# Gated linear attention and a multiplicative FFN on one core: q and k of chunks 2 to 8 issued by GpSimd, the decays' rows stored from ScalarE's queue

## The chip, the cores and the metric

The kernel runs on one core of a Trainium2 chip, as one launch. The metric is the device time of the launch in microseconds (us). A profile is one execution of its own. It names the engines PE (TensorE matmuls), PEld (TensorE weight loads), DVE (VectorE), ACT (ScalarE), POOL (GpSimd) and SP (SyncE, which here only issues DMAs). A "q" behind a name (SPq, POOLq) is that engine's instruction queue.

## The reference

The inputs are q, k, v and alpha of shape (batch 4, heads 8, 768 positions, 48 values), and four float64 weight matrices. The first half is a recurrence over the positions of each head, the second half a gated feed-forward layer with two further products:

```python
for t in range(S):
    state = alpha[:, :, t, :, None] * state + np.einsum('bhd,bhe->bhde', k[:, :, t], v[:, :, t])
    y[:, :, t] = np.einsum('bhd,bhde->bhe', q[:, :, t], state)
x = y.transpose(0, 2, 1, 3).reshape(B * S, H * D)      # (3072, 384)
out = ((x @ w1) * (x @ w2) @ w3) @ w_out               # (3072, 384)
```

## The kernel before

**Chunks.** The 768 positions of a batch are cut into 6 chunks of 128, so there are 24 chunks `n` = 0 to 23. A chunk's tile has the 128 positions on the partitions and 8 heads by 48 values along each partition. In memory, 48 values of one head at one position lie together (192 bytes), so each load of alpha, k, q or v of a chunk (192 KB) consists of 1,024 pieces of 192 bytes.

**What is done for a chunk.** `logs(n)` takes the logarithm of alpha on ScalarE (L272). `decays(n)` sums the logarithms over the positions with one matmul (L287) and makes two tiles `e` with Exp (L293, L294). `decayed(n)` multiplies k and q with them on VectorE (L303, tile `qk`). `transposed(n)` turns `qk` over on TensorE (L325), and ScalarE copies it out (L327, tile `qkT`). `scores(n)` multiplies keys and queries (L365), VectorE masks the product (L368, tile `ms`), `outer(n)` makes the chunk's contribution to the state (L337, added at L345 or L347), and `attend` and `attend_state` give y (L391, L385), which ScalarE copies out (L395, tile `x`) and SP stores to a scratch tensor `xd`.

**Rows for the state.** Between two pairs of chunks the state has to be decayed. For this, three rows of 384 values are stored to a small tensor `ends` in memory: a row of alpha (L279, in `logs`) and two rows of `e` (L296 and L298, in `decays`). `load_ends` reads them back as single values on partitions (L311, two DMAs, tile `dec`), and `advance` multiplies them together and onto the state on GpSimd (L354 to L356, tile `T`). This is done for chunks 2, 4, 8, 10, 14, 16, 20 and 22. All these DMAs are issued by GpSimd.

**Weights.** w1 and w2 come as float64 in tiles of 128 by 512 (`raw`, 512 KB, L192). `to_fp32` and `load_gates` convert a tile in several steps on ScalarE (L200, L205, L217) and VectorE (L201, L204, L207, L208, L210, L219). The first six tiles are needed before the first gate can start.

**Order of the work.** The loop over `n` (L600) writes one step per chunk. Step `n` holds the scores of chunk `n`, the transposes of `n + 1`, `decayed(n + 2)`, `decays(n + 3)` and `logs(n + 4)`; in the first six steps (`n < FIRST`) it also holds about one weight tile's conversion. Each engine works through its own instructions in order. A tile scheduler sets that order; `after_marks(...)` keeps an instruction behind a named one. `mark["pool"]` names an instruction of GpSimd behind which the loads of v are put. From step 5 on, the matmuls of the gates (L421, 18 or 9 at a time) are mixed in. A gate of the first group needs the first three chunks' `xd`, loaded as `xT` (L407) and split by `split_x` (L413 on ScalarE, L414 and L415 on VectorE), and the first six weight tiles. After the attention come the remaining gates, the product of w3 and w_out (the "fold") and the last product.

**Loads and their queues.** SP issues, in program order, alpha (L132), k and q (L138, L139), v of chunks 0 to 2 and from 8 on (L144), `raw` (L192), the stores of `xd` (L262) and more. GpSimd issues v of chunks 3 to 7. alpha and kq have three buffers each, so kq of chunk `n + 3` can start only when `decayed(n)` has read chunk `n`, and alpha of chunk `n + 3` only when `logs(n)`, and the store of alpha's row where there is one, have read chunk `n`. `raw` has four buffers. Each DMA signals its end on one of eight semaphores for the DMAs of SP and ScalarE, or of eight for those of GpSimd, taken in turn; so an issue waits until the DMA that had the same semaphore eight issues earlier has landed.

Of the kernel before, what the change touches and what calls it, by code (L numbers as in the profile page):

```python
# [48 lines left out]
def kernel(  # L49
# [12 lines left out]
    nc = tc.nc  # L62
    B, H, S, D = q.shape
    C = 128
# [5 lines left out]
    DP = 64  # L70
# [32 lines left out]
    def bank():  # L103
        return ps.tile([C, 512], FP32, tag="bank", name="bank")

    st, mark = {}, {}

    def after_marks(*names):
        stack = ExitStack()
        for x in names:  # L110
            stack.enter_context(tc.issue_after(mark[x]))
        return stack
# [4 lines left out]
    ends = {n: dram.tile([3, DM], FP32, name=f"ends{n}") for n in range(2, N, 2) if n % NCH}  # L117
# [7 lines left out]
    def rows(src, n):  # L125
        b, c = divmod(n, NCH)
        return src[b, :, ds(c * C, C), :].rearrange("h p d -> p h d")

    def load_a(n):
        if n < N:  # L130
            st["a", n] = inp.tile([C, H, D], FP32, tag="ac", name="ac")
            nc.sync.dma_start(out=st["a", n], in_=rows(alpha, n))  # L132

    def load_kq(n):
        if n >= N:
            return
        st["kq", n] = inp.tile([C, 2, H, D], FP32, tag="kq", name="kq")
        nc.sync.dma_start(out=st["kq", n][:, 0], in_=rows(k, n))  # L138
        nc.sync.dma_start(out=st["kq", n][:, 1], in_=rows(q, n))  # L139

    def load_v(n):
        if n < N:
            st["v", n] = vs[n % len(vs)]
            (nc.gpsimd if 2 < n < 8 else nc.sync).dma_start(out=st["v", n][:, :, 0:D], in_=rows(v, n))  # L144

    nc.scalar.preload_act_table_set(LN_EXP_SET)
    load_a(0)
# [20 lines left out]
    decs = [p1.tile([C, 3, NP], FP32, name=f"dec{i}") for i in range(2)]  # L168
# [68 lines left out]
    def fetch(ahead=3):  # L237
        while weights and len(begun) < ahead:
            begun.append(weights.popleft())
            next(begun[-1])  # L240
# [17 lines left out]
    def store():  # L258

        while later:  # L260
            dst, src = later.popleft()
            nc.sync.dma_start(out=dst, in_=src)  # L262
# [4 lines left out]
    def logs(n):  # L267
        if n >= N:
            return
        a = st.pop(("a", n)).rearrange("p h d -> p (h d)")  # L270
        la = st["la", n] = work.tile([C, DM], FP32, tag="la", name="la")
        nc.scalar.activation(la, a, AF.Ln)  # L272
        if n >= LATE:

            t = st["la", n] = work.tile([C, 2, DM], FP32R, tag="la2", name="la2", bufs=1)
            nc.scalar.copy(t[:, 0], la)
            nc.vector.tensor_sub(t[:, 1], la, t[:, 0].bitcast(FP32))
        if n in ends:
            nc.gpsimd.dma_start(out=ends[n][2:3], in_=a[0:1])  # L279

    def decays(n):
        if n >= N:
            return
        lc = bank()[:, 0:DM]
        la = st.pop(("la", n))
        if n < LATE:
            nc.tensor.matmul(lc, sums[:, n % 2].bitcast(FP32), la, start=True, stop=True)  # L287
        else:
            for i in range(2):
                nc.tensor.matmul(lc, sums[:, n % 2], la[:, i], start=(i == 0), stop=(i == 1))  # L290

        e = st["e", n] = work.tile([C, 2, DM], FP32, tag="e", name="e", bufs=3)
        nc.scalar.activation(e[:, 0], lc, AF.Exp, scale=-1.0)  # L293
        mark["e", n] = nc.scalar.activation(e[:, 1], lc, AF.Exp).ins  # L294
        if n in ends:
            mark["pool"] = nc.gpsimd.dma_start(out=ends[n][0:1], in_=e[0:1, 0]).ins  # L296
        if n + 1 in ends:
            mark["pool"] = nc.gpsimd.dma_start(out=ends[n + 1][1:2], in_=e[C - 1:C, 1]).ins  # L298
        load_ends(n)

    def decayed(n):
        if n < N:
# [3 lines left out]
    def load_ends(n):  # L306
        if n not in ends:
            return
        with nc.allow_non_contiguous_dma(reason="single values to partitions"):
            for i in range(2):  # L310
                nc.gpsimd.dma_start(out=decs[n // 2 % 2][ds(DP * i, D)].rearrange("d m j -> d (m j)"),  # L311
                                    in_=ends[n].rearrange("m (j i d) -> i d (m j)", i=2, d=D)[i])

    def transposed(n):
        if n >= N:
# [58 lines left out]
    def attend_state(n):  # L374
        qkT = st.pop(("qkT", n))

        y = [bank()[:, 0:HP * C].rearrange("p (j c) -> p j c", c=C) for _ in range(2)]
        st["y", n] = y, [(half * HP + j, i, y[i][ds(DP * half, DP), j, :])  # L380
                         for j in range(HP) for i in range(2) for half in range(2)]
        if n % NCH:
            for j, i, to in st["y", n][1]:
                r = ds(DP * i, D)
                nc.tensor.matmul(to, Ts[n % 2][r, j, :], qkT[r, 1, j, :],  # L385
                                 start=(j % HP == 0), stop=False, skip_group_check=True)
# [18 lines left out]
    def load_x(g, queue=nc.sync):  # L405
        st["xT", g] = xp.tile([C, KM, TG], FP32, tag="xT", name="xT")
        queue.dma_start(out=st["xT", g], in_=xd[g].rearrange("(k p) t -> p k t", p=C))  # L407

    def split_x(g, i):
        x = st.pop(("xT", g))  # L410
        t = tr[i].tile([C, 3, KM, TG], FP32R, tag="x3", name="x3")
        st["x3", g] = t
        nc.scalar.activation(t[:, 0], x, AF.Copy, scale=1.0 - 2.0 ** -13)  # L413
        nc.vector.tensor_sub(t[:, 1], x, t[:, 0].bitcast(FP32))  # L414
        mark["x3"] = nc.vector.scalar_tensor_tensor(t[:, 2], t[:, 0].bitcast(FP32), -1.0 - 1.0 / P, x,  # L415
                                                    op0=ALU.mult, op1=ALU.add).ins
# [73 lines left out]
    def gate(g, f):  # L490
        yield from (late_gate if late else early_gate)(g, f)
# [104 lines left out]
    FIRST = 6  # L596
# [3 lines left out]
    for n in range(N + 1):  # L600
        store()
        if n in loads:
            load_x(loads[n])
        load_a(n + 5)
        raws = (3, 3, 3, 3, 2, 2, 3, 3)[n] if n < 8 else 4
        for m in (n + 3,) * (n <= FIRST) + (n + 4,) * (n >= FIRST):
            load_kq(m)
            if n < FIRST - 2:
                fetch(raws)
            if n >= FIRST:  # L610
                load_v(m - 1)
        if n:
            attend_state(n - 1)
        if n < N:
            scores(n)
        transposed(n + 1)
        if n < FIRST:
            with after_marks("pool"):
                load_v(n + 2)
        if n - 2 in begin and n > FIRST:  # L620
            g, tiles = begin[n - 2]
            with after_marks(("ms", n), ("qkT", n + 1)):
                split_x(g, 0)
            fill.extend(gate(g, f) for f in tiles)
        pieces = (3, 3, 2, 0)[(n - FIRST) % 4] if n >= FIRST else 0
        if n == 0:
            with after_marks(("qkT", 0)):
                logs(2)
            decays(2)
            with after_marks(("e", 2)):  # L630
                logs(3)
        early, ready = n < FIRST, len(thirds) if n > 2 else n // 2
        marks = (*[("qkT", n + 1)] * (n < N - 1), *[("qk", n + 1), ("ms", n)] * early, *["x3"] * (n - 2 in begin and n > FIRST))
        if n < N - 2:
            with after_marks(*marks):
                convert(2 if n == 0 else 1, raws)
        advance(n)
        if n:
            attend(n - 1)
        outer(n)  # L640
        third(ready)
        run(pieces > 0)
        if early:
            with after_marks(*marks):
                convert(1, raws)
        with after_marks(*[("ms", n)] * (n < 3)):
            decayed(n + 2)
        if not early:
            with after_marks(*[("qkT", n + 1)] * (n < N - 4)):
                logs(n + 4)  # L650
        if n == 4:
            load_x(0)
        convert(early and n > 0, raws)
        run(pieces > 1)
        decays(n + 3)
        if early:
            with after_marks(("e", n + 3)):
                logs(n + 4)
        if n < N - 2:
            convert(early or n % 3 == 0, raws)  # L660
        if n == FIRST - 1:
            assert len(done) == 2 * KM
            g, tiles = begin[n - 2]
            with after_marks("l"):
                split_x(g, 0)
            fill.extend(gate(g, f) for f in tiles)
        run(pieces > 2)
        if n == N - 3:
            while begun:
                convert(1)  # L670
            weights.extend(load_out(j) for j in range(KF))
            fetch(4)
# [91 lines left out]
```

## Time and profile before

| what | value |
|---|---|
| median of 3 runs | 476.67 us (474.95 to 478.01) |
| the profiled execution: its own time | 476.57 us |
| its span, first to last instruction | 474.8 us |
| PE busy | 456.5 us, 96% of the span |
| DVE, ACT, POOL busy | 359.1, 279.6, 76.6 us |
| DMA packets under 512 bytes | 99,360 of 148,783 |
| load of k or q of a chunk, 192 KB: issue to landing | 5.7 us in the median |
| load of `raw`, 512 KB: issue to landing | 5.2 us in the median |

The times of a profile count from the span's start. A "busy" engine is one with an instruction running; PE's busy time is modelled, since matmuls overlap. In the timeline view a row holds the start, the busy time, engine, line, operation, the tiles (written <- read), the count, and in brackets how long the engine had been idle before and what ended that. In the view of stages, a row gives each engine's busy time within a window, then the clock that TensorE was granted (1.00 is full), the share of time in which the 16 DMA engines had packets (packets overlap, so it can be over 1), and the rate in GB/s.

### The profile page before, as it was taken

Reading aid. Unit: us, or ns where it says so; the run is one execution under the profiler, and the core shown is the slowest. Engines: PE = TensorE matmul, PEld = TensorE weight load, DVE = VectorE, ACT = ScalarE, POOL = GpSimd, SP = SyncE. Lnnn points to the kernel's source line nnn. Section 1 sums busy time; section 2 is a strip of 40 time slices with the busy share of each in tenths; the row PEclk is TensorE's granted clock in tenths of the full one; section 3 lists DMA queues with packets and bytes.
Section 4 is the critical chain, followed back from the end, with each engine's and each line's share of the span. In section 5 each row is a group of like instructions: output and inputs, shape, how many; then the busy total and the mean of one; then the engine's idle time right before and its main releaser. Section 6 shows DMA issues by size and latency. Waiting matters only on the chain.

```text
span 474.8 us, 10017 instructions
## 1 busy us (share of the span) xinstructions
PE 456.5 (96%) x3836; PEld 432.7 (91%) x3836; DVE 359.1 (76%) x578; ACT 279.6 (59%) x555; POOL 76.6 (16%) x144
## 2 busy tenths in 40 slices
PE   4878899999999999999999999999999999999997
PEld 2666689899999998999999999999999999999996
DVE  2778796899979888999999868855542876666761
ACT  4668765768668563988877675654543533333330
POOL 3433122104201310121221202111011000000000
PEclk9988899999999999999999999999999999999999
DMA  9999999999899944467685532202012976555511
GB/s 179 216 209 189 228 187 247 221 239 224 184 221 206 240 142 136 137 207 251 204 271 164 182 128 84 99 35 101 33 51 88 257 233 191 163 166 174 177 51 50
DMA packets 148783, 80.29 MB, mean 169 GB/s; under 512 B 99360, under 2 KB 140576, under 8 KB 148736
## 3 DMA queue, kind: packets, MB, share of 16 engines
q1 hardware_dynamic: 142960, 64.44, 55.5%
q0 software_dynamic: 5776, 15.22, 10.2%
q8 instruction: 30, 0.49, 0.5%
q14 instruction: 17, 0.14, 0.1%
HBM read 57.58 MB, written 22.06 MB: 168 GB/s over the span
## 4 chain that ended last, share of the span: by engine, by line
PE 85%; DMA 5%; DVE 4%; ACT 2%; issue 1%; SPq 1%; POOL 1%; DVEq 0%; ACTq 0%; POOLq 0%
PE bank L421 70%; PE bank L365 4%; DMA kq<-in_q_dram 4%; PE bank L391 3%; PE bank L325 2%; PE bank L385 2%; PE bank L523 1%; PE bank L337 1%; PE bank L287 1%; DMA xT<-xd 1%; PE bank L290 1%; DVE qk L303 1%; DVE ms L368 1%; DVE x L415 1%; SPq L262 1%
## 5 line engine op out<-in xcount | busy, mean ns | idle before, releaser
L421 PE MATMUL bank<-x,w 128*128 128x384 f32 x1152 | 212.6, 338 | 1.1 <-DVE x L415 0.6
L421 PEld LDWEIGHTS bank<-x,w 128*128 128x128 f32 x1152 | 200.2, 188 | 4.0 <-PE bank L421 0.9
L421 PE MATMUL bank<-w3o,ab 128*128 128x384 f32 x576 | 100.2, 336 | 0.0
L421 PEld LDWEIGHTS bank<-w3o,ab 128*128 128x128 f32 x576 | 99.9, 188 | 0.0
L446 ACT ACTIVATE bank<-bank 128x384 f32<-128x384 f32 x96 | 45.7, 476 | 41.2 <-PE bank L421 40.6
L430 ACT ACTIVATE t<-bank 128x384 f32<-128x384 f32 x64 | 31.5, 494 | 57.4 <-PE bank L421 56.2
L496 POOL DMA_DIRECT2D abd<-ab x45 | 26.3, 583 | 144.9 <-DVE ab L482 126.2
L482 DVE TENSOR_TENSOR ab<-bank,r 128x384 f32<-128x384 f32 x44 | 24.4, 554 | 24.9 <-ACT bank L446 15.9
L552 DVE TENSOR_TENSOR ab<-abl,ab 128x1024 fp32r<-128x1024 f32 x24 | 29.4, 1224 | 12.3 <-ACT ab L551 12.3
L327 ACT COPY qkT<-bank 128x512 f32<-128x512 f32 x48 | 25.8, 590 | 20.5 <-PE bank L325 20.5
L551 ACT ACTIVATE ab<-abl 128x1024 fp32r<-128x1024 f32 x24 | 25.4, 1060 | 20.2 <-PE bank L421 18.3
L421 PE MATMUL bank<-wo,w3T 128*128 128x384 f32 x192 | 35.9, 334 | 0.0
L303 DVE TENSOR_TENSOR qk<-kq,e 128x768 f32<-128x768 f32 x24 | 22.9, 954 | 14.9 <-ACT e L294 8.3
L421 PEld LDWEIGHTS bank<-wo,w3T 128*128 128x128 f32 x192 | 33.5, 188 | 0.0
L368 DVE TENSOR_TENSOR ms<-bank,keep 128x512 int32<-128x512 int32 x48 | 31.2, 683 | 0.1
L432 DVE SCALAR_TENSOR_TENSOR o<-bank,t 128x384 f32<-128x384 f32 x24 | 13.4, 557 | 23.0 <-issue 13.7
L432 DVE SCALAR_TENSOR_TENSOR r<-bank,t 128x384 f32<-128x384 f32 x40 | 22.1, 554 | 11.4 <-ACT t L430 8.5
L205 ACT ACTIVATE power<-power,rebias 128x512 uint32<-128x512 uint32 (+1 forms) x36 | 25.1, 699 | 9.2 <-DVE power L204 9.0
L365 PEld LDWEIGHTS bank<-qkT 48*128 48x128 f32 x384 | 24.4, 193 | 6.3 <-issue 3.0
L365 PE MATMUL bank<-qkT 48*128 48x128 f32 x384 | 29.3, 291 | 0.4 <-ACT x L395 0.4
L553 DVE SCALAR_TENSOR_TENSOR ab<-ab,abl 128x1024 fp32r<-128x1024 f32 x24 | 29.2, 1218 | 0.0
L391 PE MATMUL bank<-ms,v 128*64 128x128 f32 x384 | 27.6, 289 | 0.0
(81 smaller groups left out, 578.9 us busy)
## 6 DMA issues: line engine op xcount, KB each, us to landing
raw<-in_moe_w_dram SPq DMA_DIRECT2D x28, 512.0 KB, 5.2
abl<-abd SPq DMA_DIRECT2D x24, 512.0 KB, 4.4
abd<-ab POOLq DMA_DIRECT2D x45, 192.0 KB, 2.8
xT<-xd POOLq DMA_DIRECT2D x9, 576.0 KB, 4.5
ac<-in_alpha_dram SPq DMA_DIRECT2D x24, 192.0 KB, 5.2
kq<-in_k_dram SPq DMA_DIRECT2D x24, 192.0 KB, 5.7
kq<-in_q_dram SPq DMA_DIRECT2D x24, 192.0 KB, 5.7
xd<-x SPq DMA_DIRECT2D x48, 96.0 KB, 4.0
```

Source lines behind the costliest of these rows:

```text
L303: mark["qk", n] = nc.vector.tensor_mul(qks[n % 3][:, :, :, 0:D], st.pop(("kq", n)), st.pop(("e", n)).rearrange("p i (h d) -> p i h d", h=H ...
L327: mark["qkT", n] = nc.scalar.copy(qkT[:, :, :, ds(DP * half, DP)], tp[half]).ins
L365: nc.tensor.matmul(sc[i][:, j, :], qkT[r, 0, j, :], qkT[r, 1, j, :], start=True, stop=True)
L368: masked = nc.vector.tensor_tensor(ms[:, i].bitcast(I32), sc[i].bitcast(I32), keep_bc, op=ALU.bitwise_and)
L391: nc.tensor.matmul(to, vc[:, 2 * j + i, :], ms[:, i, j, :], start=(n % NCH == 0 and j % HP == 0), stop=(j % HP == HP - 1), skip_group_chec ...
L421: nc.tensor.matmul(p, w[part][i], x[part][i], start=start and part == parts[0] and i == 0, stop=stop and part == parts[-1] and i == n - 1, ...
L430: nc.scalar.activation(t, p1, AF.Copy, scale=(1.0 + 1.0 / P) * scale)
L432: nc.vector.scalar_tensor_tensor(to, p2, scale, t, op0=ALU.mult, op1=ALU.add)
L446: nc.scalar.activation(p, p, AF.Copy, scale=1.0 + 1.0 / P)
L496: (nc.gpsimd if late else nc.sync).dma_start(out=abd[g][:, f, :], in_=ab)
L552: nc.vector.tensor_sub(t[:, 1], ab, t[:, 0].bitcast(FP32))
L553: nc.vector.scalar_tensor_tensor(t[:, 2], t[:, 0].bitcast(FP32), -1.0 - 1.0 / P, ab, op0=ALU.mult, op1=ALU.add)
```

## The change

1. k and q of chunks 2 to 8 are issued by GpSimd instead of SP. In steps 0 to 5, `load_kq(n + 3)` stands where `load_v(n + 2)` stood, behind GpSimd's mark; the mark is now set by each kq and v load and by the loads of `dec`.
2. For chunks below 9 the three rows are stored by DMAs in ScalarE's queue instead of GpSimd's. These are 9 DMAs, since chunks 2, 4 and 8 have such rows.
3. `load_ends` is called for chunk `n + 1` in step `n`, instead of at the end of `decays`.
4. The raw weight tiles are fetched at the step's start without kq loads between.

```diff
     def load_kq(n):
...
-        nc.sync.dma_start(out=st["kq", n][:, 0], in_=rows(k, n))
-        nc.sync.dma_start(out=st["kq", n][:, 1], in_=rows(q, n))
+        queue = nc.gpsimd if 1 < n < 9 else nc.sync
+        queue.dma_start(out=st["kq", n][:, 0], in_=rows(k, n))
+        x = queue.dma_start(out=st["kq", n][:, 1], in_=rows(q, n))
+        if 1 < n < 9:
+            mark["pool"] = x.ins
 
     def load_v(n):
         if n < N:
             st["v", n] = vs[n % len(vs)]
-            (nc.gpsimd if 2 < n < 8 else nc.sync).dma_start(out=st["v", n][:, :, 0:D], in_=rows(v, n))
+            x = (nc.gpsimd if 2 < n < 8 else nc.sync).dma_start(out=st["v", n][:, :, 0:D], in_=rows(v, n))
+            if 2 < n < 8:
+                mark["pool"] = x.ins
...
         if n in ends:
-            nc.gpsimd.dma_start(out=ends[n][2:3], in_=a[0:1])
+            (nc.scalar if n < 9 else nc.gpsimd).dma_start(out=ends[n][2:3], in_=a[0:1])
...
         if n in ends:
-            mark["pool"] = nc.gpsimd.dma_start(out=ends[n][0:1], in_=e[0:1, 0]).ins
+            (nc.scalar if n < 9 else nc.gpsimd).dma_start(out=ends[n][0:1], in_=e[0:1, 0])
         if n + 1 in ends:
-            mark["pool"] = nc.gpsimd.dma_start(out=ends[n + 1][1:2], in_=e[C - 1:C, 1]).ins
-        load_ends(n)
+            (nc.scalar if n < 9 else nc.gpsimd).dma_start(out=ends[n + 1][1:2], in_=e[C - 1:C, 1])
...
-                nc.gpsimd.dma_start(out=decs[n // 2 % 2][ds(DP * i, D)].rearrange("d m j -> d (m j)"),
-                                    in_=ends[n].rearrange("m (j i d) -> i d (m j)", i=2, d=D)[i])
+                mark["pool"] = nc.gpsimd.dma_start(out=decs[n // 2 % 2][ds(DP * i, D)].rearrange("d m j -> d (m j)"),
+                                    in_=ends[n].rearrange("m (j i d) -> i d (m j)", i=2, d=D)[i]).ins
...
         raws = (3, 3, 3, 3, 2, 2, 3, 3)[n] if n < 8 else 4
-        for m in (n + 3,) * (n <= FIRST) + (n + 4,) * (n >= FIRST):
+        if n < FIRST - 2:
+            fetch(raws)
+        for m in (n + 3,) * (n == FIRST) + (n + 4,) * (n >= FIRST):
             load_kq(m)
-            if n < FIRST - 2:
-                fetch(raws)
-            if n >= FIRST:
-                load_v(m - 1)
+            load_v(m - 1)
...
         if n < FIRST:
-            with after_marks("pool"):
+            with after_marks(*["pool"] * ("pool" in mark)):
+                load_kq(n + 3)
                 load_v(n + 2)
+        load_ends(n + 1)
```

In the built programs, the order of PE's instructions is the same before and after. On SP, 14 loads are gone. On ACT, 9 DMA issues are added. On GpSimd, 14 loads are added and 9 stores are gone: its order is now k and q of chunk 2, k, q of 3 and v of 3, k and q of 4, `dec` of 2, k, q of 5 and v of 4, `advance(2)`, k, q of 6 and v of 5, `dec` of 4, v of 6, k and q of 7, `advance(4)`, k and q of 8, v of 7. On ACT, the alpha row of chunk 4 is stored between the conversion step L217 of weight tile 0 and the copy of `qkT` of chunk 2, and by the turn of the semaphores its issue waits for the landing of weight tile 2; the first row of `e` of chunk 4 is stored ahead of `logs(5)` and waits for the landing of alpha of chunk 5.

## The prediction

> **What bounds the kernel now.** I first asked from when TensorE is never idle, with the waits of PE in two windows, 0 to 62 us and 60 to 180 us (from 180 us to the end that view is empty). First answer, then second:
>
> ```profile
> PE bank L325 <- DVE qk L303: 5.7, 4, 2.0
> PE bank L287 <- POOL dec L185: 4.3, 1, 4.3
> ```
> ```profile
> PE bank L421 <- DVE x L415: 0.6, 1, 0.6
> PE bank L421 <- ACT qkT L327: 0.3, 1, 0.3
> ```
>
> The 0.6 us end at 60.45 us, when the first gate's twelve matmuls start behind the split of x. From there PE runs 474.8 − 60.45 = 414.35 us nearly without a gap, in an order that the change leaves alone. So only the first 60 us can move the time. What they wait for is in VectorE's timeline:
>
> ```profile
> 23.03 0.96 DVE L303 TENSOR_TENSOR qk<-kq,e 128x768 f32<-128x768 f32 x1 [0.61 <-DMA kq<-in_q_dram]
> ...
> 31.25 0.96 DVE L303 TENSOR_TENSOR qk<-kq,e 128x768 f32<-128x768 f32 x1 [2.13 <-DMA kq<-in_q_dram]
> ...
> 38.89 0.96 DVE L303 TENSOR_TENSOR qk<-kq,e 128x768 f32<-128x768 f32 x1 [0.16 <-DMA kq<-in_q_dram]
> ...
> 46.60 0.96 DVE L303 TENSOR_TENSOR qk<-kq,e 128x768 f32<-128x768 f32 x1 [1.31 <-DMA kq<-in_q_dram]
> ...
> 53.68 0.96 DVE L303 TENSOR_TENSOR qk<-kq,e 128x768 f32<-128x768 f32 x1 [2.25 <-DMA kq<-in_q_dram]
> ```
>
> Five waits for q, 6.46 us together: what earlier q and k could save. Is q late because SP issues it late, or because the DMA engines have no time? The stages (columns: width; PE, PEld, DVE, ACT, POOL busy; clock; DMA share; GB/s) answer:
>
> ```profile
> 4.00:6.00 2.00, 1.62 (x2) 0.50 (x2) 0.00 (x0) 0.20 (x2) 0.23 (x3) 1.00 1.40 199
> 6.00:8.00 2.00, 0.09 (x2) 0.09 (x4) 0.96 (x1) 1.39 (x3) 0.00 (x0) 1.00 1.49 173
> 8.00:10.00 2.00, 2.00 (x18) 1.34 (x18) 0.00 (x0) 0.94 (x2) 0.00 (x0) 1.00 1.46 189
> ...
> 44.00:46.00 2.00, 1.84 (x33) 1.40 (x32) 1.29 (x3) 2.00 (x6) 0.48 (x1) 1.00 0.62 105
> ```
>
> The DMA engines are full from 2 us on; only a few dips (44 to 46 us) are the queue's fault. At 173 to 199 GB/s a 192 KB load takes about 1.05 us of all engines; for a 512 KB weight tile I take 1.8 us (291 GB/s, the rate of the stage from 30 to 32 us, where 4 KB pieces prevail). Then SP's order is a first-come queue. Counted from 2.0 us, with 0.5 us for landing: alpha of chunk 4 has 13 loads and 2 tiles up to itself, 2.0 + 13.65 + 3.6 + 0.5 = 19.75 us; ScalarE's timeline says 19.80:
>
> ```profile
> 19.80 0.52 ACT L272 ACTIVATE la<-ac 128x384 f32<-128x384 f32 x1 [1.52 <-DMA ac<-in_alpha_dram]
> ```
>
> q of chunk 3 has 16 loads and 2 tiles, 22.9 us; seen 23.03. q of chunk 4 has 21 loads, 3 tiles and about 1.1 us of xd and dec, 31.05 us; seen 31.25. The model holds to 0.2 us three times: up to 31 us the kernel is bound by the DMA engines, and a load comes earlier only if another comes later.
>
> **What the Trainium skill says.** "DMA: Bandwidth & Descriptors", section "Issuing engines are not separate DMA queues": DMAs of all issuers run on the same 16 engines and interleave; a second issuer saves only issue time. The three sums above agree. Same page, "Queues, rings and completion order": an engine takes turns between queue rows, a whole packet at a time. The trace shows what this does to small pieces: while a v load of GpSimd (q0) meets SP's 192-byte pieces (q1), from 26 to 27 us, 43 packets carry more than 351 do:
>
> ```profile
> q0 software_dynamic: 43, 0.12, 68.7%
> q1 hardware_dynamic: 351, 0.07, 66.7%
> ```
>
> So GpSimd's loads overtake SP's, with some 60% of the bytes. Same page, "SWDGE vs HWDGE vs iDMA": GpSimd's descriptors are made in software. Seen: 0.93 us to issue a v load, and its bytes start 2 to 3 us after the issue.
>
> **The change part by part.**
>
> *q and k to GpSimd.* 14 loads leave SP, where k of chunks 2 to 8 took about 8.3 us and q 15.7 us of issue, mostly stalled. GpSimd pays 14 × 0.93 = 13.0 us and loses 9 stores of 0.52 us, 4.7; it was busy 20.5 of the first 64 us, so this fits. k and q of chunk 2 go at 4.2 us instead of 9.2; they stood ahead of alpha 4 anyway. k and q of chunk 3 can go when qk of chunk 0 ends (7.87 us), with v of chunk 3 behind; those of chunk 4 after qk of chunk 1, about 15 us. So by alpha 4 there are now five more loads on the engines: 5 × 1.05 = 5.25, and alpha 4 lands at 19.8 + 5.2 = 25.0. The price of a GpSimd load is not shown alone. From 26 to 27 us its packets took 0.687 us for 0.12 MB, so 1.12 us a load; from 41 to 42 us, beside larger pieces, 0.445 us for 0.14 MB, 0.62 us. With the latter alpha 4 lands 2.2 us sooner. I take the slow end, since its company is 192-byte pieces.
>
> *What waits behind it.* ScalarE takes `logs(4)` in order, and behind it stand w of tile 0 and the copy of qkT of chunk 2, which began at 20.75 us, 0.95 us after `logs(4)`. Then comes the new store of alpha's row, which waits for weight tile 2: one tile behind alpha 4, so 25.0 + 1.8 = 26.8. With the store's issue qkT of chunk 2 starts near 27.45 us, 6.7 us late. The next store waits for alpha 5 (20 loads, 3 tiles, 0.5 us of dec: 29.4 us), when ScalarE gets there at about 31 us: nothing. VectorE and PE wait for ScalarE here.
>
> *What is won back.* q and k of chunks 4 to 8 are then there before they are wanted: chunk 5 is issued behind `dec` of chunk 2 (about 27 us, wanted at 41), chunk 6 behind `advance(2)` (31.5, wanted near 47), chunks 7 and 8 about 39 and 43. So the waits behind qkT of chunk 2 go: 2.13 + 0.16 + 1.31 + 2.25 = 5.85 us. In the steps without a wait for q VectorE needed 6.0 to 6.5 us, as they will be.
>
> *Stores on ScalarE.* 9 issues; SP's shortest cost 0.33 to 0.37 us, so 3 us of ScalarE, from nothing (it waits for loads anyway) to 3 us. Cover: its waits for alpha and, at 55 us, 1.4 us for xT. I take nothing beyond the stall counted; the range has the rest.
>
> *Rows loaded one step ahead.* From chunk 10 on GpSimd's order is in effect as before; PE waited 0.5 us in all for `T`. Nothing; if `dec` came late, PE's L385 would wait, with the state used a step later. *SP's other loads* (raw, alpha, xd) move up in its queue; alpha 7 now waits for the store of alpha 4's row, about 31.5 us, and lands near 41, wanted near 43: nothing, but close.
>
> Sum: +6.7 − 5.85 = +0.85 us. Against the profiled span 474.8 + 0.85 = 475.65 us; the median lies 476.67 − 474.8 = 1.87 us above the span, so 477.5 us.
>
> **The rivals.**
>
> *Faster: the waits go and nothing comes in their place.* For it: DMA dips like 44 to 46 us, caused by SP standing behind weight tiles that wait for a buffer, and the cheap price of 0.62 us. Against it: the full engines up to 31 us. It gives 476.67 − 6.46 = 470.2 us.
>
> *Slower: the 6.7 us stay.* The place is the chain ScalarE, PE, VectorE in steps 2 to 5: with q there, another link ends last, since ScalarE and VectorE each have about 6 us of work a step and PE is granted half clock for part of the time (0.66 on average from 30 to 40 us). If only 1 us of the 5.85 is won back: 476.67 + 5.7 = 482.4 us. It decides from less than 1.9 us won back, which is 1% slower.
>
> *No effect.* The change does not get the loads forward: q and k on GpSimd stand behind dec and advance, which waited up to 5.2 us each for rows, and land when they did. For it: the row's way through memory, 4 us each way. Against it: chunks 3 and 4 stand ahead of all that. 476.7 us.
>
> **How the numbers follow.** Forecast 0.50, own range 474 to 480.5 (the cheap GpSimd price below, 3 us of ScalarE above); faster 0.17; slower 0.23; no effect 0.10. A measurement tells 1%, 4.8 us, from no change: below 471.9 is faster, above 481.4 slower. Most of the faster rival is below and nearly all of the slower above, a little of the forecast at each side: faster 0.15, same 0.63, slower 0.22. For 8 in 10 the range goes to 471.5 and 482.5.
>
> **What would show it.** In the profile after: VectorE's wait for q under 1.5 us in the first 62 us; ScalarE's wait for alpha up from 3.4 to 8 us or more, the longest ahead of `logs(4)` at about 25 us; qkT of chunk 2 at about 27.5 us; first gate's run of twelve near 61.3 instead of 60.45 us, and no idle PE after. It is wrong if alpha of chunk 4 lands before 22 us (then GpSimd's loads do not displace SP's, and the kernel gets faster), or if the steps behind it stay at 7 us (then slower).

## The result and the profile after

The changed kernel takes 483.48 us (median of 5 runs, 483.31 to 483.80) against 476.67: a ratio of 1.0145 with the interval 1.0120 to 1.0169. It is slower, by more than the forecast's range allowed. The profiled execution took 483.36 us; its span is 481.6 us, 6.8 us longer than before.

All of that arises before the first gate. First the waits of PE from 60 to 180 us (releaser: total us, times, longest), then the twelve matmuls behind the split of x in PE's timeline, before and after:

```profile
PE bank L369 <- ACT qkT L331: 4.3, 1, 4.3
PE bank L425 <- DVE x L419: 0.6, 1, 0.6
```
```profile
60.45 2.34 PE L421 MATMUL bank<-x,w 128*128 128x384 f32 x12 [0.56 <-DVE x L415]
```
```profile
67.48 2.33 PE L425 MATMUL bank<-x,w 128*128 128x384 f32 x12 [0.57 <-DVE x L419]
```

They start 7.03 us later, and no wait follows. What remains of the span, 481.6 − 67.48 = 414.1 us, is what remained before (414.35). VectorE's qk rows, of chunks 1, 3, 4, 5, 6 and 8:

```profile
12.47 0.96 DVE L307 TENSOR_TENSOR qk<-kq,e 128x768 f32<-128x768 f32 x1 [4.47 <-DMA kq<-in_q_dram]
...
27.32 0.95 DVE L307 TENSOR_TENSOR qk<-kq,e 128x768 f32<-128x768 f32 x1
34.00 0.94 DVE L307 TENSOR_TENSOR qk<-kq,e 128x768 f32<-128x768 f32 x1
37.05 0.95 DVE L307 TENSOR_TENSOR qk<-kq,e 128x768 f32<-128x768 f32 x1
46.74 0.95 DVE L307 TENSOR_TENSOR qk<-kq,e 128x768 f32<-128x768 f32 x1
...
63.23 0.96 DVE L307 TENSOR_TENSOR qk<-kq,e 128x768 f32<-128x768 f32 x1 [0.38 <-ACT e L299]
```

The waits for q behind chunk 1 are gone. VectorE's qk is ahead of before at chunk 5 (37.05 against 38.89) and still at chunk 7 (52.14 against 53.68), but at chunk 8 it is behind (63.23 against 60.49). These rows flatter the change, since qk now stands further forward in VectorE's queue. The chain itself shows in ScalarE's copies of qkT, of chunks 4, 5 and 6, first before, then after:

```profile
34.98 1.06 ACT L327 COPY qkT<-bank 128x512 f32<-128x512 f32 x2
...
41.45 1.08 ACT L327 COPY qkT<-bank 128x512 f32<-128x512 f32 x2 [0.24 <-PE bank L325]
...
48.74 1.05 ACT L327 COPY qkT<-bank 128x512 f32<-128x512 f32 x2
```
```profile
37.71 1.05 ACT L331 COPY qkT<-bank 128x512 f32<-128x512 f32 x2
...
46.75 1.10 ACT L331 COPY qkT<-bank 128x512 f32<-128x512 f32 x2
...
59.18 1.05 ACT L331 COPY qkT<-bank 128x512 f32<-128x512 f32 x2
```

They are 2.7, 5.3 and 10.4 us late: behind chunk 4 the kernel loses again. The stages say that the DMA engines stayed full where they had a dip (same columns as in the prediction):

```profile
44.00:46.00 2.00, 2.00 (x29) 2.00 (x28) 1.36 (x2) 2.00 (x6) 2.00 (x3) 0.50 1.08 237
```

What holds the copies up is seen in ScalarE's timeline ("ACTq" rows are its DMA issues):

```profile
24.56 0.52 ACT L277 ACTIVATE la<-ac 128x384 f32<-128x384 f32 x1 [2.15 <-DMA ac<-in_alpha_dram]
...
27.41 1.07 ACT L331 COPY qkT<-bank 128x512 f32<-128x512 f32 x2 [1.81 <-DMA raw<-in_moe_w_dram]
...
42.95 0.37 ACT L399 COPY x<-bank 128x256 f32<-128x256 f32 x1 [3.63 <-DMA xd<-x]
...
53.59 0.21 ACTq L303 DMA_DIRECT2D ends<-e  x1
53.85 0.52 ACT L277 ACTIVATE la<-ac 128x384 f32<-128x384 f32 x1 [1.22 <-DMA raw<-in_moe_w_dram]
...
58.11 1.16 ACT L417 ACTIVATE x<-xT 128x1152 fp32r<-128x1152 f32 x1 [3.74 <-DMA xT<-xd]
```

The first two rows are the forecast's stall, to within 0.5 us. The other three waits are new or longer (before: none for xd, none for a weight tile ahead of a store, 1.43 us for xT), 8.6 us together. And the last row stands at another place in ScalarE's queue. Before, `rest` of the sixth weight tile, which the first gate needs as well as the split, ran ahead of the split:

```profile
49.68 0.68 ACT L200 ACTIVATE rest<-raw 128x512 f32<-128x512 uint32 x1
...
55.22 1.17 ACT L413 ACTIVATE x<-xT 128x1152 fp32r<-128x1152 f32 x1 [1.43 <-DMA xT<-xd]
```

Now it runs behind it, at 60.12 us. VectorE, whose own part of the split still comes behind the sixth tile's w (and now behind qk of chunk 8 too), waits for it:

```profile
60.83 0.69 DVE L212 SCALAR_TENSOR_TENSOR mant<-mant,rest 128x512 f32<-128x512 uint32 x1 [4.58 <-ACT rest L205]
...
64.71 1.35 DVE L418 TENSOR_TENSOR x<-xT,x 128x1152 fp32r<-128x1152 f32 x1
```

From ScalarE's part of the split to VectorE's passed 57.68 − 55.22 = 2.46 us before and pass 6.60 us now. No line of the diff asks for this: the order within each queue is planned when the kernel is built, and the move of q and k changed it (in e1 below, which leaves q and k on SP, `rest` runs ahead of the split as before; in e2, which moves them, behind it).

### The profile page after: what moved, and what is told of

The parts are those of the page before. It is cut to its first block, busy times and chain, and to the rows that moved or that the text cites. A ratio compares the mean times of both kernels' runs of the same rounds, so it can differ in the third digit from the quotient of the medians.

```text
span 481.6 us, 10026 instructions
## 1 busy us (share of the span) xinstructions
PE 457.0 (95%) x3836; PEld 434.4 (90%) x3836; DVE 359.3 (75%) x578; ACT 279.9 (58%) x555; POOL 84.0 (17%) x149
## 4 chain that ended last, share of the span: by engine, by line
PE 86%; DMA 8%; ACT 2%; SPq 1%; DVE 1%; issue 1%; ACTq 0%; DVEq 0%
PE bank L425 70%; PE bank L395 4%; PE bank L369 4%; DMA raw<-in_moe_w_dram 4%; DMA xd<-x 2%; PE bank L389 2%; PE bank L329 2%; PE bank L527 1%; DMA ac<-in_alpha_dram 1%; PE bank L341 1%; PE bank L295 1%; DMA xT<-xd 1%; ACT qkT L331 1%; SPq L132 1%; DVE qk L307 0%
## 5 line engine op out<-in xcount | busy, mean ns | idle before, releaser
L369 PEld LDWEIGHTS bank<-qkT 48*128 48x128 f32 x384 | 26.8, 210 | 14.0 <-ACT qkT L331 6.2
L369 PE MATMUL bank<-qkT 48*128 48x128 f32 x384 | 32.0, 310 | 7.4 <-ACT qkT L331 4.6
L556 DVE TENSOR_TENSOR ab<-abl,ab 128x1024 fp32r<-128x1024 f32 x24 | 29.4, 1224 | 12.4 <-ACT ab L555 12.3
L212 DVE SCALAR_TENSOR_TENSOR mant<-mant,rest 128x512 f32<-128x512 uint32 (+1 forms) x36 | 23.6, 655 | 6.7 <-ACT rest L205 6.7
```

The lines of the kernel that those rows point to most:

```text
L369: nc.tensor.matmul(sc[i][:, j, :], qkT[r, 0, j, :], qkT[r, 1, j, :], start=True, stop=True)
L556: nc.vector.tensor_sub(t[:, 1], ab, t[:, 0].bitcast(FP32))
```

## The experiments

One table for the 18 further kernels. The second column is the ratio to the kernel before, timed beside it; the third is the time, in each one's profile, at which VectorE's part of the split starts. From this mark to the end of the span pass 416.5 to 418.4 us in each of them. But it is one execution, and executions of one kernel differ: the profiled one is 1.2 us above the kernel's median in e1 and 1.0 to 1.7 us below it in e3, e11, e12, e13 and e19. So a difference of a microsecond or two in the third column alone shows little, and the ratio decides. One of e17's 14 executions took 1542 us; its ratio leaves it out.

| kernel | ratio [95%] | split on VectorE, us |
|---|---|---|
| before | 1 | 57.68 |
| the changed kernel | 1.0145 [1.0120, 1.0169] | 64.71 |
| e1: row stores alone | 1.0017 [1.0006, 1.0028] | 60.69 |
| e2: q and k alone | 1.0173 [1.0152, 1.0194] | 65.58 |
| e3: ScalarE's split behind w | 1.0129 [1.0093, 1.0166] | 62.48 |
| e4: xd stored by ScalarE | 1.0165 [1.0142, 1.0188] | 65.68 |
| e5: tiles and alpha held behind xT | 1.0083 [1.0053, 1.0113] | 63.73 |
| e6: and q, k of chunk 8 | 1.0137 [1.0106, 1.0168] | 64.05 |
| e8: GpSimd for chunks 2 to 4 | 1.0112 [1.0082, 1.0142] | 63.91 |
| e9: GpSimd for chunks 5 to 8 | 1.0151 [1.0114, 1.0187] | 66.59 |
| e10: order | 1.0067 [1.0041, 1.0094] | 62.70 |
| e12: order, rows by GpSimd | 1.0061 [1.0042, 1.0080] | 60.88 |
| e11: order, hold | 1.0071 [1.0053, 1.0089] | 60.57 |
| e13: order, hold, rows by GpSimd | 1.0048 [1.0029, 1.0068] | 59.63 |
| e14: three x buffers | 1.0138 [1.0107, 1.0170] | 65.32 |
| e15: order, three x buffers | 1.0064 [1.0044, 1.0084] | 62.12 |
| e16: order, hold, three x buffers | 1.0012 [0.9997, 1.0028] | 59.10 |
| e17: e16, rows by GpSimd | 1.0047 [1.0027, 1.0067] | 60.21 |
| e18: e15, chunk 8's rows by GpSimd | 1.0044 [1.0026, 1.0061] | 58.92 |
| e19: e16, alpha 4 ahead of tile 2 | 1.0024 [1.0011, 1.0036] | 57.74 |

**First: which part of the change, and which wait.** e1 undoes the move of q and k (their two loads on SP, at their old place in the step), e2 the row stores (all three on GpSimd). e3 and e4 leave both parts in.

```diff
 e3:  mark["w"] = nc.scalar.activation(h, w, AF.Copy, ...).ins      # in load_gates
-            with after_marks("l"):
+            with after_marks("l", "w"):
                 split_x(g, 0)
 e4, in store(), for what steps 0 to 6 store:
-            nc.sync.dma_start(out=dst, in_=src)
+            nc.scalar.dma_start(out=dst, in_=src)
```

> Only the rows' part of the change: stored from ScalarE's queue, read back one step ahead of use; q and k stay with SP. If the loss comes from the loads that GpSimd puts in front of SP's (theory D), this is about the kernel before: 476 to 478 us, with alpha of chunk 4 landing near 19.8 us and the copy of x never waiting for xd. If it comes from the stores on ScalarE, whose issue waits for a bulk load eight issues back and on whose landing SP's alpha loads wait (theory S), it is 480 us or more, with waits of 1 us or more in ScalarE's queue at the stores.

> Only q and k by GpSimd, with the row stores left with GpSimd (read back one step ahead, as in the changed kernel). Theory D: the start is as late as in the changed kernel, alpha of chunk 4 near 24.5 us and xT near 58 us, so 482 to 486 us. Theory S: the stores are off ScalarE, so 476 to 478 us.

> The changed kernel with ScalarE's part of the first split of x queued behind the last weight conversion of the first six, instead of ahead of it. In the changed kernel the split waited 3.7 us for xT at 58.1 us and held back that conversion, which took until 64.7 us. If that order is what turned a late xT into a late gate (theory O), the conversion is done by 59 us, the split of x follows xT at once, and the first full gate starts near 62 to 63 us instead of 67.5: 478 to 479.5 us. If the order only shows the lateness and the work is late anyway (theory D alone), 482 us or more.

> The changed kernel with the stores of xd of the first chunks issued from ScalarE's queue instead of SP's, so that they need not stand behind weight tiles and alpha there. Theory D: xd lands in 4 to 5 us instead of up to 10, the 3.6 us wait of the copy of x goes, and xT comes 2 to 4 us sooner: 478 to 480.5 us. Theory O without D: the split still stands ahead of the conversion and little moves, 482 to 484 us.

e1 against e2 settles the first point: the row stores by themselves cost 0.17%, and the move of q and k by itself costs as much as both. Yet alpha of chunk 4 did not land where e1's expectation put it: `logs(4)` began at 22.22 us, not near 19.8, and in e1's profile the split comes 3.0 us later than before. In e2 ScalarE issues no store and never waits for one; instead it waits 6.4 us for xT, and the time is no better. In e4 the wait for xd shrinks from 3.63 to 1.17 us and nothing is gained: ScalarE then stands 4.15 us at 56 us for a weight tile. So a stall that goes is replaced by another, later one. Each edit also lets the queues be planned anew: in e4 ScalarE's part of the split came to stand behind the sixth tile's w by itself. e3 gains 2.2 us of profile, but its ratio can't be told from the changed kernel's.

**Second: loads ahead of need, or the early delay?** By the time xT was issued, the changed kernel had loaded two more weight tiles, an alpha and a chunk of q and k. e5 queues the tiles and the alpha behind xT ("the hold"), e6 q and k of chunk 8 too; e8 and e9 split the move in two.

```diff
 e5, in load_a and to_fp32 (mark["xT"] is set by load_x):
-            nc.sync.dma_start(out=raw[:, ds(i * m, m)], in_=src)
+            with after_marks(*["xT"] * ("xT" in mark and not late)):
+                nc.sync.dma_start(out=raw[:, ds(i * m, m)], in_=src)
 e8:
-        queue = nc.gpsimd if 1 < n < 9 else nc.sync
+        queue = nc.gpsimd if 1 < n < 5 else nc.sync
 e9:                      4 < n < 9
```

> SyncE keeps the 7th and 8th weight tile and alpha of chunk 10 behind the load of xT. Theory 'loaded ahead of need': 2 x 1.8 + 1.05 = 4.65 us of DMA time leave the stretch before xT, so xT is issued near 50 us instead of 53.82, the first gate's twelve start near 64 instead of 67.48, and the time is about 480 us (478.5 to 481.5). Rival 'early displacement' (alpha of chunk 4 lands 5 us late and nothing gives that back): these loads are later than the damage, so the twelve start near 67 and the time stays at 483 to 484 us.

> As the run before, and q and k of chunk 8 go back to SyncE, behind the load of xT too. 'Loaded ahead of need': another 2 x 1.05 = 2.1 us leave the stretch, all 6.75 us are gone: the twelve near 61 to 62 us, 477 to 479 us. 'Early displacement': 483 to 484 us, as without the hold.

> GpSimd issues q and k of chunks 2 to 4 alone; SyncE those of 5 to 8, as before. 'Early displacement': all five early loads still overtake alpha of chunk 4, so logs(4) stays near 24.5 us and the time at 482 to 484 us. 'Loaded ahead of need': the loads of chunks 5 to 8 keep SyncE's tiles back again, xT is issued near 50 us, and the time is 477.5 to 480 us although logs(4) stays late.

> The other half: SyncE issues q and k of chunks 2 to 4, GpSimd those of 5 to 8. 'Early displacement': logs(4) is back near 20 us and the time near 477 us. 'Loaded ahead of need': logs(4) is early, but the tiles and q, k of chunk 8 still come ahead of xT; the first stretch's 2.7 us are not lost, the rest is: 479.5 to 482.5 us.

e8 fits early displacement (`logs(4)` at 24.71 us, and three quarters of the loss). e9 seems to refute it, with `logs(4)` at 21.79 us and no gain, but is not clean: its qk of chunk 4 stands 7.3 us, put down to q, which SP now issues at 29.43 us, and starts at 42.96 instead of 34.00. In e2, with the rows on GpSimd ahead of q and k, alpha lands sooner, `logs(4)` begins at 20.79 us, and the loss is the same; but e2 has a stall of its own (VectorE waits 3.62 us, until 35.14, for GpSimd's `T`). What settles it is e16, further below: there the early delay is all there (`logs(4)` at 24.92 us, qkT of chunk 2 at 28.05 against 20.75) and hardly any loss. So the early delay is not what the loss consists of. The hold gives something in e5 (1.0083) and next to nothing in e6. e6 was forecast at 477 to 479 us if loads ahead of need cost DMA time and nothing else, and took 483.91. Its xT came when it came before the change (ScalarE's row, then two of VectorE's):

```profile
54.87 1.17 ACT L420 ACTIVATE x<-xT 128x1152 fp32r<-128x1152 f32 x1 [1.19 <-DMA xT<-xd]
```
```profile
61.30 0.43 DVE L209 TENSOR_SCALAR mant<-raw 128x512 uint32<-128x512 uint32 x1 [2.41 <-DMA raw<-in_moe_w_dram]
...
64.05 1.35 DVE L421 TENSOR_TENSOR x<-xT,x 128x1152 fp32r<-128x1152 f32 x1
```

Yet VectorE's split started 9.2 us later: in its queue two operations of the seventh tile, which I had just held back, stood ahead. So e6 does not clear the loads of blame, and it points to the order.

**Third: the order.** e10 puts ScalarE's part of the split behind the sixth tile's w, and on VectorE qk of chunk 8 and the seventh tile's first two operations behind the split. e12, e11 and e13 add the row stores on GpSimd, the hold of e5, and both.

```diff
 e10: e3's edit, and
-        with after_marks(*[("ms", n)] * (n < 3)):
+        with after_marks(*[("ms", n)] * (n < 3), *["x3"] * (n == FIRST)):
             decayed(n + 2)
 and in to_fp32, for `top` and `power`:
+        with after_marks(*["x3"] * ("x3" in mark and not late)):
```

> Places in the queues put back: ScalarE's part of the split stands behind the sixth conversion's w, and on VectorE qk of chunk 8 and the seventh tile's first two operations stand behind the split. Theory 'queue order' (ScalarE's copy of xT stands ahead of rest of the sixth tile, so that tile, which the first gate needs too, starts 5 us late): VectorE's split starts at 60 to 61.5 us instead of 64.71, the twelve at 63 to 64, 479 to 480.5 us. Rival 'ScalarE's chain' (its waits for xd and for the row's store from 38 to 56 us make qkT of chunk 6 late, and all else follows it): the split stays past 62.4 us as with the split behind w alone, 481.5 to 483 us.

> As the run before, with the rows stored by GpSimd again, so that ScalarE issues no DMA. 'Queue order': no more than 1 us sooner than with the stores on ScalarE, 478.5 to 480 us. 'ScalarE's chain': the stall behind the row's store (2 to 4 us at 53 to 56 us) goes and the twelve come 2 to 3 us sooner, about 479 us, or, if xT is what it then waits for, nothing changes: 481 to 482 us.

> Places put back as in the first run of this call, and the 7th and 8th tile and alpha of chunk 10 held behind xT, where VectorE no longer asks for the 7th tile ahead of the split. 'Queue order' plus 'loaded ahead of need': xT about 2 to 3 us sooner than without the hold, the twelve near 61 to 62, 477 to 478.5 us. If loads ahead of need cost nothing: the same time as the first run.

> Order, hold, and rows stored by GpSimd. If the three account for the loss between them: 476 to 478 us, as the kernel before. If the wait for xd (3.6 us of ScalarE at 39 to 43 us) is a loss by itself, it stays: 479 to 480.5 us.

The order returns about half: 1.0067 against 1.0145, and the intervals are apart. e10 fell between its two forecasts: 481.24 us, with the split at 62.70, later than 'queue order' allowed. It moves three things; the first alone is e3 (1.0129), so by the medians most of the gain needs those on VectorE, though the two intervals just touch. Adding the hold (e11) or the stores (e12) does not show in the ratios, and with both (e13) the time, 480.43 us, is where it was expected if the wait for xd is a loss by itself. What all four share in their profiles is ScalarE's wait for xd ahead of the copy of x: 4.89 us in e10, 3.09 in e12, 3.21 in e11 and 1.12 in e13.

**Fourth: take that wait away.** Three x buffers, and two e buffers for the room; what the second edit does alone was not tried.

```diff
-        x = work.tile([C, HP, 2, C], FP32, tag="x", name="x")
+        x = work.tile([C, HP, 2, C], FP32, tag="x", name="x", bufs=3)
-        e = st["e", n] = work.tile([C, 2, DM], FP32, tag="e", name="e", bufs=3)
+        e = st["e", n] = work.tile([C, 2, DM], FP32, tag="e", name="e", bufs=2)
```

> The changed kernel with three x buffers (and two of e). ScalarE's wait of 3.6 us at 39 to 43 us goes. Theory 'two losses in turn' (the wait for xd, then the queue order): ScalarE reaches its copy of xT 3 us sooner, but SyncE's xT is no more than 2 to 3 us sooner (xd of chunk 2 is stored sooner by what the wait was), so the twelve start at 64 to 65.5 and the time is 480.5 to 482 us. Rival 'only the order counts': as the changed kernel, 483 to 484 us.

> Order put back and three x buffers. 'Two losses in turn': both go, VectorE's split at 58 to 59.5 us, 476.5 to 478.5 us, as the kernel before. If another link takes the place of the wait: 480 to 481.5 us, as with the order alone.

> Order, the hold of tiles and alpha behind xT, and three x buffers. 'Two losses in turn': the hold adds nothing that can be told from the run before, 476 to 478 us. If the loads ahead of need are a loss that the others cover: 1 us or more below the run before.

> As the run before with the rows stored by GpSimd. ScalarE's stalls behind the row's store (qkT of chunk 2 at 27.5 us, 2 us) go, but q and k of chunk 5 come later, behind dec: within 1 us of the run before, 475.5 to 478 us. This is the version with the best prospect of beating the kernel before; if the DMA engines' full first 31 us set the end, it can't be under 476.

The wait is gone in e14 and gives nothing (1.0138), nor in e15 (1.0064 against e10's 1.0067): I was wrong on both. But with the hold as well it is worth 0.6% (e16 1.0012 against e11 1.0071, intervals apart; the profiles show 1.5 us of the 2.8), and e16 can't be told from the kernel before. e15's profile shows what had taken the wait's place, SP's issue first, then ScalarE:

```profile
49.37 0.39 SPq L197 DMA_DIRECT2D raw<-in_moe_w_dram  x1
```
```profile
54.02 0.20 ACTq L305 DMA_DIRECT2D ends<-e  x1
54.27 0.52 ACT L279 ACTIVATE la<-ac 128x384 f32<-128x384 f32 x1 [3.79 <-DMA raw<-in_moe_w_dram]
```

The first store of chunk 8's rows stood in ScalarE's queue until the eighth weight tile, issued at 49.37 us, had landed. A store of 1.5 KB that takes 0.20 us to issue held up ScalarE 3.79 us, because the DMA that used its semaphore last was that tile.

**Fifth: is it that store?**

```diff
 e18 (e15 and:), in logs and decays, n < 7 for the row of chunk n + 1
-        (nc.scalar if n < 9 else nc.gpsimd).dma_start(...)
+        (nc.scalar if n < 8 else nc.gpsimd).dma_start(...)
 e19 (e16 and:)
     load_a(3)
+    load_a(4)
     load_kq(2)
     decayed(1)
     fetch(2)
     load_v(1)
-    load_a(4)
```

> Order, three x buffers, and the three row stores of chunk 8 by GpSimd; no hold. 'The store waits for the 8th tile': ScalarE no longer stands at 50 to 56 us, VectorE's split is 2 to 3 us sooner than 62.12, 477.5 to 479 us. 'DMA time taken by loads ahead of need': xT stays as late as 54.3 us and the time at 480 to 481 us.

> Order, hold, three x buffers, and alpha of chunk 4 issued by SyncE ahead of weight tile 2 and v of chunk 1. logs(4) should come 2 to 2.9 us sooner (22 to 22.9 us). If what is left of the loss starts there, qkT of chunk 2 is 1.5 to 2.5 us sooner and the time 475.5 to 477 us. If the store of alpha's row, which waits for a weight tile that is now 1 us later, takes its place, qkT of chunk 2 stays near 28 us and the time at 478.

In the profiles it is: without any hold the split starts at 58.92 us, 3.2 us sooner than in e15, and xT is issued at 50.67 instead of 54.26. The time is within the forecast for it (478.11 us), but in the ratios the step is 0.2%, and the intervals overlap (1.0064 and 1.0044). e18's PE, beside e16's:

```profile
61.70 3.73 PE L427 MATMUL bank<-x,w 128*128 128x384 f32 x12 [0.57 <-DVE x L421]
```
```profile
61.87 2.32 PE L429 MATMUL bank<-x,w 128*128 128x384 f32 x12 [0.56 <-DVE x L423]
```

They start together, yet e18's twelve take 1.4 us longer: from 60 to 65 us TensorE was granted 0.66 in e18's profile and 1.00 in e16's. Whether that is behind the ratios (1.0044 and 1.0012) is not shown: the medians of the two are all but equal, 478.11 and 477.97, and the kernel before took 476.44 beside e18 and 477.34 beside e16. In e19's profile `logs(4)` is at 22.56 us and the twelve start at 60.51, level with before (60.45), but it is the fastest of 22 executions, whose median is 477.80 against 476.44. No version beats the kernel before.

## Why the prediction was wrong

**The bound was right.** Only the first 60 us moved, and PE behind the first gate did not change: 414.1 against 414.35 us.

**The displacement was right in its sum, not in its parts.** alpha of chunk 4 was forecast for 25.0 and `logs(4)` began at 24.56; the store behind a weight tile put qkT of chunk 2 at 27.41 (27.45 forecast, with 0.65 us for an issue that took 0.20). The delay of 4.76 us looks like five loads at 0.95, near the price taken (1.05). e1 says otherwise: there q and k stay with SP, of the five loads only v of chunk 3 goes early (4.15 us instead of 22.69), and still

```profile
22.22 0.52 ACT L274 ACTIVATE la<-ac 128x384 f32<-128x384 f32 x1 [2.88 <-DMA ac<-in_alpha_dram]
```

is `logs(4)`, 2.4 us late. So the four loads of q and k add 2.3 us, 0.6 each if the parts add up, which is the cheap price (0.62); e8 against e9 (24.71 and 21.79 us) gives 0.7. What makes up e1's 2.4 us was not looked into. That the sum came out within 0.5 us is in part luck. "Issuing engines are not separate DMA queues", the section of the Trainium skill's page "DMA: Bandwidth & Descriptors" that the forecast leaned on, agrees with e8 and e9: loads that GpSimd issued earlier put SP's alpha back.

**The waits for q went, as forecast, but not what followed from it.** Of the 6.7 us qkT of chunk 4 (37.71 us against 34.98) had 2.7 left, so 4.0 were back by then. The step that failed is the sum "+6.7 − 5.85": it took the waits off VectorE and let nothing come in their place after chunk 4. Instead of the 0.85 us left by the sum, the first gate came 7.03 us late. With what came in their place removed (e16) the twelve start at 61.87 us, 1.4 us late, although qkT of chunk 2 is as late as forecast. What came, by the runs:

- *"SP's other loads (raw, alpha, xd) move up in its queue ... nothing, but close"* was wrong. Two weight tiles were loaded ahead of xT that came behind it before, and stores to xd landed in 5.7 to 10.2 us instead of 3.9 to 5.4, and ScalarE stood 3.63 us for a free x buffer. With order and hold in place that wait is worth 0.6% (e11 to e16).
- *"Stores on ScalarE ... nothing beyond the stall counted"* was wrong for chunk 8's. I had worked out for chunk 4 that a store waits for a weight tile, and did not carry it to 50 us, where the tile had moved up. It is 3.2 us between two profiles (e15 to e18) and 0.2% in the ratios, where it is not clear of noise. Alone, with SP's tiles at their old place, the stores cost 0.17% (e1), within what was forecast.
- The queue orders were not looked at in the forecast beyond PE's. ScalarE's copy of xT now stood ahead of the sixth tile's `rest`. Both orders could have been read before the run. Putting it back, with three operations of VectorE, is worth 1.0145 to 1.0067, some 3.7 us of the median; ScalarE's place alone is not clear of noise (e3).

These do not add up one by one: an x buffer alone gives nothing, ScalarE without stores (e2) nothing, the order half, since the next stall holds ScalarE up in place of the one removed. The page "PSUM — Partial Sum Buffer" of the skill, section "Engine vs sequencer instructions", says that ScalarE's and VectorE's queues are strictly first in, first out; the traces agree, with 3.79 us of ScalarE in e15 and 2.41 us of VectorE in e6 behind a DMA that the work next in line did not need. With order, hold and x buffer together, and so without the store's wait too, the kernel is level with before (e16).

**The rivals.** The faster one failed on its own sign: `logs(4)` came at 24.56 us, not before 22. The slower one, that the 6.7 us stay in steps 2 to 5, was right in sign and size (482.4 us) and wrong in place: 4.0 us were won back there, and were lost again, with more, from 39 to 64 us, so that its size came out is luck. "No effect" failed, since the waits for q did go. Of the signs named, the sum of the waits for alpha (8.8 us) and qkT of chunk 2 came true; the longest of these waits was not ahead of `logs(4)` (2.15 us) but of `logs(3)` (3.00 us), and the twelve did not come at 61.3 us; for q the waits behind chunk 1 are gone, but chunk 1's own, which the forecast left out, is 4.47 us. Its qk starts at 12.4 to 12.9 us wherever GpSimd loads chunk 2 early, and at 11.5 to 11.9 where SP does (before, e1, e9).

**What stays open.** Why e17, with the rows on GpSimd, is slower than e16 was not pursued (VectorE waits 1.78 us there for q of chunk 5, behind the rows on GpSimd, and 1.6 of the 2.7 us between the spans lie behind the split). How the loss divides between the loads' DMA time, the semaphores and the planned order is known only for the sets of edits tried. The 1.36 us that e19's profile gains over e16's do not show in its ratio. The gain of the order, 2.0 us between the profiles and 3.7 between the ratios, is known to no better than that.

## What to carry to other kernels

A load that comes earlier on a full DMA engine also lets everything behind it in the old queue come earlier, needed or not; list what those loads will overtake, which buffer and semaphore each will hold, and who stands behind it. Print the order of every engine's queue before and after, not only of the engine that is the bound: an operation that waits for a late DMA must not stand ahead of work that another path needs. And when one stall is removed without effect, look for the next one in the same queue before calling the first harmless: here three edits had to go together.

## What the runs showed of the hardware

- The issue of a row's store on ScalarE takes 0.20 us in most cases (0.47 for the first), yet in this program it holds the queue for as long as its semaphore's last user is in flight: 3.79 us in e15.
- After PE waits of 1.2, 0.6 and 0.6 us around the first gate e18's profile shows a granted clock of 0.66 from 60 to 65 us, and its twelve matmuls took 3.73 us; after waits of 0.2, 0.9 and 0.6 us e16's shows 1.00, and 2.32 us. Each is one execution, and what makes the difference was not measured.
- SP's stores of x (96 KB each) from 25 to 60 us landed in 5.7 to 10.2 us beside GpSimd's loads of q and k, against 3.9 to 5.4 us before.
